# Polysketch attention followed by an ELU feed-forward layer: the order of the first loads, sketch products and features

## The chip, the cores and the metric

The kernel runs on one core of a Trainium2 chip. The metric is device time in microseconds of one execution. Below, "the profile" and "the trace" are of one execution, recorded by the hardware profiler; times in it count from the start of its span. PE is TensorE's matmuls, DVE is VectorE, ACT ScalarE, POOL GpSimd, SP SyncE (which issues most DMAs). All arithmetic is in float32.

## The reference, cut to what matters

q, k and v have the shape (4, 4, 1088, 32): 4 batches, 4 heads, 1088 positions, head dimension 32. S1 and S2 are (8, 32), w_in is (128, 2048), w_out (2048, 128). The sketches and the weights come in as 64-bit floats, q, k and v as float32.

```python
def phi(x):
    a = np.einsum('rd,bhsd->bhsr', S1, x)
    b = np.einsum('rd,bhsd->bhsr', S2, x)
    return np.einsum('bhsi,bhsj->bhsij', a, b).reshape(*x.shape[:-1], r * r)
q_p, k_p = (phi(q), phi(k))
kv = np.einsum('bhsf,bhsd->bhfd', k_p, v)
z = np.sum(k_p, axis=2)
num = np.einsum('bhsf,bhfd->bhsd', q_p, kv)
den = np.einsum('bhsf,bhf->bhs', q_p, z)[..., None] + 1e-06
x = num / den                      # then to (4352, 128)
h = x @ w_in
g = np.where(h > 0.0, h, 1.0 * (np.exp(np.minimum(h, 0.0)) - 1.0))
return g @ w_out
```

## The kernel before, in words

The order of the work on each engine is written out by hand: the program is in manual schedule, and each engine carries out its instructions in the order in which the code emits them. Waits between engines follow from the tiles that are written and read. A tile of a pool with n buffers waits until the n-th tile before it under the same tag has been read.

**Tokens and groups.** The 4352 tokens are cut into half tiles of 64 (17 per batch), and eight of these make a group: groups 0 to 8, the last one smaller. The FFN runs over groups, and in each over 8 pairs cp of 128-column chunks of the hidden layer. One step (g, cp) has two matmuls h = w_in x (`mm1`, L606), two activations per half on ScalarE (`elu_a`, L622 and L624), one VectorE operation per half (`elu_d`, L630, writes gg) and two matmuls with w_out that add into o (`mm2`, L643), two steps behind. The loop at L801 does this for all steps and hangs the attention of batches 1 to 3 and of later groups between them. Everything ahead of it, L680 to L727, is the head: it works out batch 0's keys and the first two groups, and starts the FFN.

**Loads.** SP issues nearly all. The order is S1, k and q of batch 0 in parts (the ScalarE queue issues S2 and the second half of k and q), then v of batch 0 (`load_v(0)`, L141, two DMAs of 288 and 256 KB), then raw w_in of pair 0 (`load_w(0, 0)`, L182, 256 KB), the tail of q of batch 0 (L183), and further weights. Each DMA signals on one of eight semaphores in turn, and one on the same semaphore waits for the one before.

**Rounding of the weights.** w_in and w_out come as 64-bit words; each float64 is turned into a float32 by five steps, `round_a` to `round_e` (L97 to L124): round_a on VectorE (L98), round_b on ScalarE (L103), round_c (two VectorE operations, L111 and L112), round_d (L116), round_e (L124, on VectorE or GpSimd). `RA(i)` and `RB(i)` are the first two for entry i of the list `order` (L163), `RC(i)` the other three. Entry 0 is w_in of pair 0, entry 1 w_in of pair 1, entries 2 and 3 their w_out.

**Sketches.** S16 holds S1 and S2 rounded, Sx their copies per head. `sps` (L250) gives Sab, the sketch matrices of all heads on the diagonal, masked on VectorE (L252). SXps (L237, in `make_SXh`) gives SXh through a copy on ScalarE (L238) and a mask on GpSimd (L239); it turns batch 0's sums into the weights of the denominators.

**The head, in its order.** `transp` (L230) turns keys and queries on VectorE. `KF(0)` (L280) multiplies 18 half tiles of keys with Sab into abp; in it, after five matmuls, stands `make_SXh`. Two ScalarE copies bring abp to abk (L297). `q1_first` (L440) is the same for the queries of group 0 (abqp, copied to abq at L449). `KO_first` (L336, VectorE) and `KO_pool` (L271, GpSimd) form the outer products kp. `Z_first` (L397): products for the sums z (zps, L349), their copy zl on ScalarE (L372), the product with SXh (Z, L377), the masked result in SW (`Z_out`, L381). `q1z_first` (L452) multiplies the queries with it (zqp), `q2_den` (L506) forms the denominators on VectorE (pw L513, den L516, L517, an L519), `q2_out` (L522) the outer products qp in two halves (L530) and takes a function `then` that is called behind the first half. `KA(0)` (L359) multiplies kp with v into kv, `KS_first` (L407) copies it (kd, L409), transposes it (L410) and copies again (kvS, L411). `q4_early` (L535) transposes qp on TensorE (qtp, L544), four at a time, and copies each four on ScalarE (qpT, L545). `q5_early` (L547) multiplies with kvS (xps, L551) and copies to xg, the FFN's x (L557): for group 0 both copies on ScalarE, for group 1 the second on VectorE. `mm1_first` (L608) is mm1 for (0, 0) in two blocks, one per half w of xg (L613). `q1_second` (L461) multiplies group 1's queries with SW (abwp, L466) and copies them to abw (ScalarE, L470); `q2(1)`, `q4_early(1)` and `q5_early(1)` follow for group 1 as for group 0.

**Fillers.** `keep_warm(n, cols)` (L214) is n matmuls of a constant tile whose result nobody reads (tile idle, L216). PSUM tiles of tag aux have two buffers: qtp, xps and abwp among them.

Of the kernel before, what the change touches and what calls it, by code (L numbers as in the profile page):

```python
# [12 lines left out]
F32 = mybir.dt.float32  # L13
# [14 lines left out]
def kernel(  # L28
# [20 lines left out]
    nc = tc.nc  # L49
    B, H, S, D = q.shape  # L50
    R = S1.shape[0]
    P = 128
# [4 lines left out]
    NT = S // 64  # L57
# [16 lines left out]
    def load_hd(eng, x, src, b, t0, t1, c=slice(0, 2)):  # L74
        if (x, b) not in hd:
            hd[x, b] = work.tile([P, 2, NT, D], F32, name="hd_" + x, tag="hd_" + x)
        eng.dma_start(hd[x, b][:, c, t0:t1, :],
                      src[b].rearrange("h (a c t) d -> (h a) c t d", a=32, c=2)[:, c, t0:t1, :])

    def load_v(b, engs=(nc.sync, nc.sync)):  # L80
        for u, eng in enumerate(engs):
            t0, t1 = u * KT, min(NT, u * KT + KT)
            r = slice(64 * u, 64 * u + 64)
            src = v[b].rearrange("h (y t) d -> y h t d", t=NT)[:, :, t0:t1, :]
            eng.dma_start(vt[b][r, :VN].rearrange("p (h t d) -> p h t d", h=H, t=KT)[:, :, :t1 - t0, :], src)
# [52 lines left out]
    load_hd(nc.scalar, "k", k, 0, KT, NT)  # L138
    load_hd(nc.sync, "q", q, 0, 0, 8, slice(0, 1))
    load_hd(nc.scalar, "q", q, 0, 0, 8, slice(1, 2))  # L140
    load_v(0)  # L141
    warm = const.tile([R, 1], F32, name="warm")
    nc.vector.memset(warm[:], 0.0)  # L143
    nc.scalar.activation(warm[:], warm[:], EXP)
# [4 lines left out]
    def load_w(cp, i):  # L149

        f = slice(2 * cp * P, (2 * cp + 2) * P)
        src = moe_w_out[f, :].rearrange("(c p) d -> p c d", p=P) if i else moe_w_in[:, f]
        if wide:
            if cp not in raw_w:
                raw_w[cp] = work.tile([P, 4 * P, 2], U32, name="raw", tag="raw", bufs=6)
            src = src.bitcast(U32)
            to = raw_w[cp][:, 2 * P * i:2 * P * i + 2 * P, :].rearrange("p c w -> p (c w)")
        else:
            to = W[:, cp, 2 * P * i:2 * P * i + 2 * P]
        nc.sync.dma_start(to.rearrange("p (c f) -> p c f", f=src.shape[-1]) if i else to, src)  # L160
# [10 lines left out]
    def RA(i):  # L171
        round_w(round_a, i)

    def RB(i):
        round_w(round_b, i)
# [4 lines left out]
        round_w(round_e, i, pool)  # L180

    load_w(0, 0)  # L182
    load_hd(nc.sync, "q", q, 0, 8, NT)  # L183
    load_w(1, 0)
    load_w(1, 1)
# [28 lines left out]
    def keep_warm(n, cols=256):  # L214
        for i in range(n):
            nc.tensor.matmul(idle[:, :cols], some[:, :P], some[:, :cols], skip_group_check=True)  # L216
# [18 lines left out]
    def make_SXh():  # L235
        xps = psum.tile([P, 512], F32, name="SXps", tag="aux")
        nc.tensor.matmul(xps[:, :FD], idr[:].rearrange("p x j -> p (x j)"), Sx[:R].rearrange("p h d -> p (h d)"))  # L237
        nc.scalar.copy(SXh[:], xps[:, :FD])  # L238
        nc.gpsimd.tensor_mul(SXh[:].rearrange("p (h d) -> p h d", h=H), SXh[:].rearrange("p (h d) -> p h d", h=H),  # L239
                             _ap(hmask[:], [[1, H], [0, D]]))  # L240
# [7 lines left out]
    keep_warm(1, 96)  # L248
    sps = psum.tile([P, 512], F32, name="sps", tag="aux")
    nc.tensor.matmul(sps[:, :2 * R], Sx[:].rearrange("p h d -> p (h d)"), ident[:2 * R, :2 * R])  # L250
    keep_warm(1)
    nc.vector.tensor_mul(Sab[:], _ap(sps[:, :2 * R], [[0, H], [1, 2 * R]]), _ap(bmask[:], [[1, H], [0, 2 * R]]))  # L252
    nc.gpsimd.tensor_copy(SW[:, :, :2, :].rearrange("p h x r -> p h (x r)"), Sab[:])
# [26 lines left out]
    def KF(b):  # L280
        ps = [psum.tile([P, 512], F32, name="abp", tag="h", bufs=4) for _ in range(2)]

        part = [(range(5), 0), (range(3), 1)]
        todo = [(i, u) for r, u in part for i in r] + [x for i in range(5, KT) for x in ((i - 2, 1), (i, 0))]
        todo += [(i, 1) for i in range(KT - 2, KT)]
        for n, (i, u) in enumerate(todo):
            if n == 5:
                make_SXh()
            nc.tensor.matmul(ps[i // 5][64 * u:64 * u + 64, 64 * (i % 5):64 * (i % 5) + 64],  # L289
                             kT[b][:, u * KT + i, :], Sab[:].rearrange("p h y -> p (h y)"),  # L290
                             skip_group_check=True, tile_position=(0, 64 * u))
        kf_ps.extend(ps)
        ab = feats[b] = work.tile([P, 2, KT, H, R], F32, name="abk", tag="abk", bufs=2)
        for j in range(2):
            t = slice(0, 5) if j == 0 else slice(5, KT)
            n = t.stop - t.start
            nc.scalar.copy(ab[:, :, t].rearrange("p x t h r -> p x (t h) r"),  # L297
                           ps[j][:, :64 * n].rearrange("p (m x r) -> p x m r", x=2, r=R))
# [98 lines left out]
    def Z_first():  # L397
        ps = psum.tile([P, 512], F32, name="zps", tag="h", bufs=4)
        for i in range(KT):
            z_tile(0, ps, i)  # L400
        zl = ZC(0, ps)
        keep_warm(1, 160)
        Z(0, ps, zl)
        Z_out(0, ps)
        keep_warm(1, 160)
# [46 lines left out]
    def q1z_first():  # L452
        p = psum.tile([P, 512], F32, name="zqp", tag="h", bufs=4)
        for i in range(4):
            for u in range(2):
                b, t = half_tile(0, 2 * i + u)
                nc.tensor.matmul(p[64 * u:64 * u + 64, i * 32:i * 32 + 32].rearrange("p (h r) -> p h r", h=H),
                                 qT[b][:, t, :], SW[:, :, 2, :], skip_group_check=True, tile_position=(0, 64 * u))
        return p[:, :128].rearrange("p (t h r) -> p h t r", t=4, h=H)
# [46 lines left out]
    def q2_den(g, zq=None):  # L506
        m = H * qn[g]
        x = abw[g][:, :m, :]
        pw = pws[g % 2]
        if zq is None:  # L510
            nc.vector.tensor_mul(pw[:, :m, :R], x[:, :, R:2 * R], x[:, :, 2 * R:3 * R])
        else:
            nc.vector.tensor_mul(pw[:, :m, :R].rearrange("p (h t) r -> p h t r", h=H),  # L513
                                 x[:, :, R:2 * R].rearrange("p (h t) r -> p h t r", h=H), zq)
        den = work.tile([P, 4 * H], F32, name="den", tag="den")
        nc.vector.tensor_reduce(den[:, :m], pw[:, :m], axis=AX, op=ADD)  # L516
        nc.vector.reciprocal(den[:, :m], den[:, :m])  # L517
        an = work.tile([P, 4 * H, R], F32, name="an", tag="an")
        nc.vector.tensor_mul(an[:, :m], x[:, :, R:2 * R], _ap(den[:, :m], [[1, m], [0, R]]))  # L519
        ans[g] = an  # L520

    def q2_out(g, parts=1, then=None):  # L522
        m = H * qn[g]
        x, an = abw.pop(g), ans.pop(g)
        qp[g] = work.tile([P, 4 * H, R, R], F32, name="qp", tag="qp", bufs=2)
        for i in range(parts):
            h = slice(i * m // parts, (i + 1) * m // parts)
            a_ = an[:, h]
            b_ = x[:, h, :R]
            nc.vector.tensor_mul(qp[g][:, h], _ap(a_, list(a_.ap[1:]) + [[0, R]]),  # L530
                                 _ap(b_, [b_.ap[1], [0, R], b_.ap[2]]))
            if then and i == 0:
                then()

    def q4_early(g):  # L535

        qpT[g] = work.tile([P, H, 2, P], F32, name="qpT", tag="qpT", bufs=2)
        for hh in range(2):
            p = psum.tile([P, 512], F32, name="qtp", tag="aux")
            for h2 in range(2):  # L540
                for m in range(2):
                    o = (h2 * 2 + m) * P
                    r = (2 * hh + h2) * 4 + 2 * m
                    nc.tensor.transpose(p[:, o:o + P], qp[g][:, r:r + 2].rearrange("p t i j -> p (t i j)"), ident[:])  # L544
            nc.scalar.copy(qpT[g][:, 2 * hh:2 * hh + 2], p[:].rearrange("p (h m s) -> p h m s", h=2, m=2))  # L545
# [59 lines left out]
        for c in cs:  # L605
            nc.tensor.matmul(hs[g, cp][c][:, :n], W[:, cp, c * P:c * P + P], xg[g][:, :n])  # L606

    def mm1_first(w):  # L608
        if w == 0:
            hs[0, 0] = [psum.tile([P, 512], F32, name="h", tag="h", bufs=4) for c in range(2)]  # L610
        for c in range(2):
            cols = [x[:].rearrange("p (m w s) -> p w m s", w=2, s=P)[:, w] for x in (hs[0, 0][c], xg[0])]
            nc.tensor.matmul(cols[0], W[:, 0, c * P:c * P + P], cols[1], skip_group_check=True)  # L613

    def elu_a(g, cp, c, parts=(0, 1)):

# [69 lines left out]
    KO_pool()  # L686
    Z_first()
    zq = q1z_first()
    q2_den(0, zq)
    q2_out(0, 2, lambda: RA(0))  # L690
    KA(0)
    KS_first()
    RB(0)
    keep_warm(1, 256)
    keep_warm(1, 128)
    q4_early(0)
    RA(1)
    RB(1)
    RC(0)
    q5_early(0)  # L700
    transp(qT, "q", 0, 8, NT)
    mm1_first(0)
    RA(2)
    RB(2)
    q1_second()
    mm1_first(1)
    RC(1)
    round_w(round_c, 2)
    elu_a(0, 0, 0)
    elu_a(0, 0, 1)  # L710
    mm1(0, 1)
# [1 line left out]
    q4_early(1)  # L713
    for c in range(2):
        elu_d(0, 0, c)
    RA(3)
    RB(3)
    round_w(round_d, 2)
# [70 lines left out]
    for g in range(2, NQ):  # L789
        n = NP * (g - 1)  # L790
# [60 lines left out]
```

## Time and profile before

| what | value |
|---|---|
| five executions, us | 282.84, 280.65, 280.34, 283.43, 283.45 |
| median, us | 282.84 |
| the profiled execution: its time | 282.84 |
| its span | 280.9 |
| instructions | 4933 |
| PE busy | 275.0 us, 98% of the span |
| PE weight loads | 139.0 us, 49% |
| DVE busy | 179.2 us, 64% |
| ACT busy | 181.6 us, 65% |
| POOL busy | 14.5 us, 5% |
| HBM read, written | 10.88 MB, 2.23 MB |
| DMA | 13.42 MB, mean 48 GB/s |

The busy time of matmuls is no measure of how well they are used: they are pipelined, and fillers count. A float32 matmul shows as two records. The chain of work that ended last is found by going back from the last instruction: at each step to what released it, or to the instruction before it on its engine. Time that an engine is on this chain is time that the span is made of. In the timelines each row has start, duration, engine, line, operation and out<-in with the shapes; rows of one kind that follow each other are merged (xN).

### The profile page before, as it was taken

How to read it: one execution, taken by the hardware profiler on the slowest of the kernel's cores; microseconds unless marked ns; L12 is line 12 of the kernel's file. 1: busy time of each engine (PE TensorE's matmuls, PEld its weight loads, DVE VectorE, ACT ScalarE, POOL GpSimd, SP SyncE). 2: the span in 40 equal slices, each digit the busy share in tenths (PEclk: the TensorE clock that was granted, in tenths of full speed). 3: DMA queues.
4: the chain of work that ended last, by engine and by line, in shares of the span. 5: the costliest groups of instructions: out<-in, count | busy, mean ns of one | idle time of the engine just before them, and what ended most of it. 6: DMA issues, size and time to landing. Idle time of an engine off the chain costs nothing.

```text
span 280.9 us, 4933 instructions
## 1 busy us (share of the span) xinstructions
PE 275.0 (98%) x1913; PEld 139.0 (49%) x1913; DVE 179.2 (64%) x336; ACT 181.6 (65%) x352; POOL 14.5 (5%) x39
## 2 busy tenths in 40 slices
PE   8989999999999999999999999999999999999995
PEld 6854444454444444444544454445444454444694
DVE  6498899996959784668545653566445744562442
ACT  2268968686566467666566666665666666667682
POOL 3500006300000000000000000000000000000000
PEclk9999999999999999999999999999999999999999
DMA  6993772200002200001000100020002000100020
GB/s 179 341 330 97 254 217 62 82 0 2 0 2 43 36 0 2 0 13 27 3 0 15 23 2 2 2 37 0 2 0 37 1 2 0 25 12 2 4 36 19
DMA packets 25638, 13.42 MB, mean 48 GB/s; under 512 B 18448, under 2 KB 23824, under 8 KB 25616
## 3 DMA queue, kind: packets, MB, share of 16 engines
q1 hardware_dynamic: 25024, 12.66, 17.8%
q10 hardware_dynamic: 592, 0.46, 0.5%
q8 instruction: 15, 0.25, 0.4%
q14 instruction: 7, 0.06, 0.1%
HBM read 10.88 MB, written 2.23 MB: 47 GB/s over the span
## 4 chain that ended last, share of the span: by engine, by line
PE 98%; ACT 1%; DVE 0%; issue 0%
PE h L606 41%; PE o L643 40%; PE ol L666 3%; PE idle L216 2%; PE kv L359 2%; PE h L572 1%; PE abp L289 1%; PE qps L572 1%; PE h L490 1%; PE h L613 1%; PE xps L551 1%; PE kfps L308 1%; PE qtp L544 1%; PE qps L490 1%; ACT qpT L545 0%; PE abwp L466 0%
## 5 line engine op out<-in xcount | busy, mean ns | idle before, releaser
L630 DVE SCALAR_TENSOR_TENSOR gg<-e,h 128x512 f32<-128x512 f32 (+1 forms) x144 | 93.0, 654 | 83.0 <-ACT e L624 82.8
L606 PE MATMUL h<-xg,W 128*128 128x512 f32 (+1 forms) x284 | 126.8, 569 | 0.1
L622 ACT ACTIVATE e<-h 128x512 f32<-128x512 f32 (+1 forms) x144 | 81.6, 567 | 64.8 <-PE h L606 64.6
L643 PE MATMUL o<-gg,W 128*128 128x512 f32 x256 | 121.5, 597 | 0.0
L624 ACT ACTIVATE e<-e 128x512 f32<-128x512 f32 (+1 forms) x144 | 87.3, 606 | 4.6
L606 PEld LDWEIGHTS h<-xg,W 128*128 128x128 f32 x284 | 53.4, 190 | 61.9 <-issue 49.7
L643 PEld LDWEIGHTS o<-gg,W 128*128 128x128 f32 x256 | 47.3, 190 | 55.6 <-issue 54.3
L530 DVE TENSOR_TENSOR qp<-an,abw 128x1024 f32<-128x1024 f32 (+1 forms) x9 | 9.3, 1047 | 0.3
L103 ACT ACTIVATE W<-W,ebias 128x256 uint32<-128x256 uint32 (+1 forms) x11 | 6.6, 603 | 3.4 <-DVE W L98 3.4
L572 PE MATMUL h<-qpT,kvq 32*32 32x128 f32 (+1 forms) x256 | 8.7, 257 | 0.0
L572 PE MATMUL qps<-qpT,kvq 32*32 32x128 f32 (+1 forms) x224 | 8.7, 271 | 0.0
L216 PE MATMUL idle<-some 128*128 128x256 f32 (+3 forms) x20 | 7.1, 487 | 1.2 <-DVE warm L143 1.2
L666 PEld LDWEIGHTS ol<-W,gg 128*128 128x128 f32 x64 | 8.1, 192 | 0.3
L563 DVE STREAM_TRANSPOSE qpT<-qp 128x1024 f32<-128x1024 f32 (+1 forms) x7 | 8.1, 1161 | 0.0
L666 PE MATMUL ol<-W,gg 128*128 128x128 f32 x64 | 8.1, 275 | 0.0
L584 ACT COPY xg<-h 128x128 f32<-128x128 f32 (+1 forms) x14 | 2.9, 261 | 7.8 <-PE qps L572 5.5
L572 PEld LDWEIGHTS h<-qpT,kvq 32*32 32x32 f32 x256 | 5.4, 103 | 4.7 <-issue 3.8
L111 DVE SCALAR_TENSOR_TENSOR W<-raw,W 128x256 uint32<-128x256 uint32 (+1 forms) x11 | 7.6, 693 | 0.0
L500 DVE STREAM_TRANSPOSE abw<-h 128x128 f32<-128x128 f32 (+1 forms) x14 | 3.5, 288 | 4.8 <-ACT xg L584 4.8
L271 POOL TENSOR_TENSOR kp<-abk 128x1024 f32<-128x1024 f32 (+1 forms) x3 | 6.5, 2165 | 1.8 <-ACT abk L297 1.8
L116 DVE SCALAR_TENSOR_TENSOR raw<-raw 128x256 f32<-128x256 uint32 (+1 forms) x11 | 6.0, 549 | 0.3
L359 PEld LDWEIGHTS kv<-kp,v 128*32 128x32 f32 x288 | 4.8, 110 | 2.3 <-issue 1.5
(115 smaller groups left out, 153.6 us busy)
## 6 DMA issues: line engine op xcount, KB each, us to landing
raw<-in_moe_w_in_dram SPq DMA_DIRECT2D x8, 256.0 KB, 5.9
raw<-in_moe_w_out_dram SPq DMA_DIRECT2D x8, 256.0 KB, 6.1
hd_k<-in_k_dram SPq DMA_DIRECT2D x3, 544.0 KB, 8.2
hd_q<-in_q_dram SPq DMA_DIRECT2D x3, 544.0 KB, 3.4
out_dram<-ob SPq DMA_DIRECT2D x40, 32.0 KB, 1.7
v<-in_v_dram SPq DMA_DIRECT2D x4, 288.0 KB, 6.5
v<-in_v_dram SPq DMA_DIRECT2D x4, 256.0 KB, 6.6
hd_k<-in_k_dram SPq DMA_DIRECT2D x1, 288.0 KB, 3.5
```

Source lines behind the costliest of these rows:

```text
L111: nc.vector.scalar_tensor_tensor(d, hi, 0x80000000, d, op0=AND, op1=OR)
L216: nc.tensor.matmul(idle[:, :cols], some[:, :P], some[:, :cols], skip_group_check=True)
L359: nc.tensor.matmul(kv[32 * h:32 * h + 32, :R * R], vt[b][:, (h * KT + i) * D:(h * KT + i + 1) * D], kp[i // 5][:, i % 5, h].rearrange("p i ...
L530: nc.vector.tensor_mul(qp[g][:, h], _ap(a_, list(a_.ap[1:]) + [[0, R]]), _ap(b_, [b_.ap[1], [0, R], b_.ap[2]]))
L563: nc.vector.transpose(qpT[g][:, :m].rearrange("p m f s -> p (m f s)"), qp[g][:, :m].rearrange("p m i j -> p (m i j)"))
L572: nc.tensor.matmul(ps[c][D * h:D * h + D, 64 * k:64 * (k + m)], kvq[r, b, f, h, :], qpT[g][r, n * h + 2 * k:n * h + 2 * (k + m), f, :], st ...
L606: nc.tensor.matmul(hs[g, cp][c][:, :n], W[:, cp, c * P:c * P + P], xg[g][:, :n])
L622: nc.scalar.activation(e, hs[g, cp][c][:, :n], RELU, scale=-1.0)
L624: nc.scalar.activation(e, e, EXP, scale=-1.0)
L630: nc.vector.scalar_tensor_tensor(gs[g, cp][:, c, :n], es[g, cp][:, c, :n], -1.0, hs[g, cp][c][:, :n], op0=ADD, op1=MAX)
L643: nc.tensor.matmul(ops[g][:, :n], W[:, cp, (2 + c) * P:(3 + c) * P], gg[:, c, :n], start=(first and c == 0), stop=(last and c == 1))
L666: nc.tensor.matmul(ops[g][i][:], gg[:, c, i * P:i * P + P], W[:, cp, (2 + c) * P:(3 + c) * P], start=(first and c == 0), stop=(last and c ...
```

## The change

Seven edits, all in the head:

- `load_v(0)` is issued behind `load_w(0, 0)` instead of ahead of it.
- `make_SXh()` is called directly behind the product sps, ahead of a filler, instead of inside `KF` after five matmuls.
- In `Z_first` the filler of 160 columns between the copy zl and the product Z is left out; the one behind Z stays.
- `RA(0)` goes from between the halves of `q2_out(0)` to ahead of `q2_den(0)`; `RB(0)` from behind `KS_first` to behind `q2_den(0)`. `q2_out` loses its argument `then`.
- Behind `RB(0)`'s old place the filler of 128 columns is left out; the one of 256 stays.
- The transposition of the rest of batch 0's queries goes ahead of `RA(1)`; `q1_second()` goes ahead of `mm1_first`, whose two blocks become one call.
- `round_c` of entry 2 goes from ahead of `elu_a(0, 0, 0)` to behind `elu_d(0, 0, c)`.

```diff
     load_hd(nc.scalar, "q", q, 0, 0, 8, slice(1, 2))
-    load_v(0)
     warm = const.tile([R, 1], F32, name="warm")
...
     load_w(0, 0)
+    load_v(0)
     load_hd(nc.sync, "q", q, 0, 8, NT)
...
     nc.tensor.matmul(sps[:, :2 * R], Sx[:].rearrange("p h d -> p (h d)"), ident[:2 * R, :2 * R])
+    make_SXh()
     keep_warm(1)
...
-        for n, (i, u) in enumerate(todo):
-            if n == 5:
-                make_SXh()
+        for i, u in todo:
             nc.tensor.matmul(ps[i // 5][64 * u:64 * u + 64, 64 * (i % 5):64 * (i % 5) + 64],
...
         zl = ZC(0, ps)
-        keep_warm(1, 160)
         Z(0, ps, zl)
         Z_out(0, ps)
         keep_warm(1, 160)
...
-    def q2_out(g, parts=1, then=None):
+    def q2_out(g, parts=1):
...
-            if then and i == 0:
-                then()
...
-    def mm1_first(w):
-        if w == 0:
-            hs[0, 0] = [psum.tile([P, 512], F32, name="h", tag="h", bufs=4) for c in range(2)]
-        for c in range(2):
-            cols = [x[:].rearrange("p (m w s) -> p w m s", w=2, s=P)[:, w] for x in (hs[0, 0][c], xg[0])]
-            nc.tensor.matmul(cols[0], W[:, 0, c * P:c * P + P], cols[1], skip_group_check=True)
+    def mm1_first():
+        hs[0, 0] = [psum.tile([P, 512], F32, name="h", tag="h", bufs=4) for c in range(2)]
+        for w in range(2):
+            for c in range(2):
+                cols = [x[:].rearrange("p (m w s) -> p w m s", w=2, s=P)[:, w] for x in (hs[0, 0][c], xg[0])]
+                nc.tensor.matmul(cols[0], W[:, 0, c * P:c * P + P], cols[1], skip_group_check=True)
...
     zq = q1z_first()
+    RA(0)
     q2_den(0, zq)
-    q2_out(0, 2, lambda: RA(0))
+    RB(0)
+    q2_out(0, 2)
     KA(0)
     KS_first()
-    RB(0)
-    keep_warm(1, 256)
-    keep_warm(1, 128)
+    keep_warm(1)
     q4_early(0)
+    transp(qT, "q", 0, 8, NT)
     RA(1)
     RB(1)
     RC(0)
     q5_early(0)
-    transp(qT, "q", 0, 8, NT)
-    mm1_first(0)
+    q1_second()
+    mm1_first()
     RA(2)
     RB(2)
-    q1_second()
-    mm1_first(1)
     RC(1)
-    round_w(round_c, 2)
     elu_a(0, 0, 0)
     elu_a(0, 0, 1)
     mm1(0, 1)
...
     for c in range(2):
         elu_d(0, 0, c)
+    round_w(round_c, 2)
     RA(3)
```

## The prediction

> **What bounds the kernel now.** I read the page's chain of work first, then that chain in order of time for the first 33 us, then the timelines of VectorE, TensorE and ScalarE over the same stretch. The page's fourth part:
>
> ```profile
> PE 98%; ACT 1%; DVE 0%; issue 0%
> PE h L606 41%; PE o L643 40%; PE ol L666 3%; PE idle L216 2%; PE kv L359 2%; PE h L572 1%; PE abp L289 1%; PE qps L572 1%; PE h L490 1%; PE h L613 1%; PE xps L551 1%; PE kfps L308 1%; PE qtp L544 1%; PE qps L490 1%; ACT qpT L545 0%; PE abwp L466 0%
> ```
>
> TensorE carries the end: behind about 26 us its matmuls (L606, L643) run back to back. So a microsecond won in the head, before the FFN runs steadily, moves all that follows and is worth one microsecond; an idle VectorE or ScalarE later is worth nothing. The change touches only the head. The chain there, in order of time (start, us, what):
>
> ```profile
> 4.49 0.54 PE sps L250 x2
> 5.02 1.15 PE idle L216 x2
> 6.17 1.26 PE abp L289 x10
> 7.43 0.72 PE SXps L237 x2
> 8.16 1.79 PE abp L289 x23
> ...
> 15.27 0.45 PE qtp L544 x4
> 15.72 0.07 issue
> 15.80 0.64 PE qtp L544 x4
> 16.44 0.02 issue
> 16.46 0.59 ACT qpT L545
> 17.06 0.04 issue
> 17.10 0.76 PE xps L551 x14
> 17.86 0.36 ACT xg L557
> 18.22 0.04 issue
> 18.26 1.13 PE h L613 x4
> 19.39 0.81 PE abwp L466 x16
> 20.20 1.06 PE h L613 x4
> 21.26 1.72 PE h L606 x4
> ```
>
> Up to 13.9 us TensorE is occupied without a gap, fillers (idle) included; from 14 to 18.3 us the chain hops between TensorE, VectorE (qp) and ScalarE. VectorE around the second product qp (start, us, line, operation):
>
> ```profile
> 14.15 0.69 DVE L530 TENSOR_TENSOR qp<-an,abq 128x512 f32<-128x512 f32 x1
> 14.76 0.29 DVE L98 TENSOR_SCALAR W<-raw 128x256 uint32<-128x256 uint32 x1
> 14.96 0.68 DVE L530 TENSOR_TENSOR qp<-an,abq 128x512 f32<-128x512 f32 x1
> ```
>
> The reader should see that RA(0) (L98) stands between the halves of qp: the second starts 0.81 us after the first, where back to back it would be 0.61 (14.76 - 14.15). Its end, 14.96 + 0.68 = 15.64, releases the second four transposes at 15.80.
>
> **The change, part by part.**
>
> *Load order.* w_in of pair 0 (256 KB) is issued ahead of v (544 KB) on SP; bytes and number of DMAs stay. DMA is at 1.0 share from 4 us on, so v lands later by about what 256 KB cost: the loads that follow land some 0.7 us apart (10.85, 11.68, 12.41, 13.15), so v's halves go from 7.67 and 8.67 to about 8.4 and 9.4. KA reads v at 12.7: over 3 us of cover. Raw w_in landed by about 9.4 before (SP's issue waiting for a semaphore came free then), and RA(0) wants it at 11.7. Both orders suffice: 0 us. If the cover were gone, KA would start later by the overshoot. The two q and w transfers behind keep their places, and nobody else on SP waits.
>
> *SXps directly behind sps.* It leaves the abp block, where it costs 0.72 on the chain, and stands ahead of the one filler, so the first abp moves from 6.17 to about 6.9. Its inputs are ready: idr at 3.42, Sx at 4.14. What abp waits for is no later: Sab ends at 5.28, the first kT piece at 5.70. Moved work alone gains 0; but abp is no longer broken up. The break spans 7.12 (last pass started) plus 0.11 (pitch) to 8.09, 0.86 us against 0.72. I take 0.14, between 0 and 0.3 (one more such changeover). POOL does SXh before SW's copy; SW is first read 12 us later.
>
> *Filler of 160 columns before Z removed.* zl ends at 11.30, Z starts at 11.44 behind the filler. Without it 0.05 remains (kd 14.24 to its transpose 14.29): 0.09, of which ScalarE's abq copy, which waits for the later end of abqp, gives up some 0.03. Bounds 0 and 0.14. SW, zqp and pw are then 0.2 earlier (pw 12.81 to 12.6).
>
> *RA(0) ahead of q2_den, RB(0) ahead of kd.* RA(0) (0.29) goes into the 0.76 us for which VectorE waits for zqp; RB(0) (0.51) into ScalarE's wait of 2.68 us ahead of kd. The halves of qp close up: 0.20. With the 0.2 above, qp ends at 15.24, and the second transposes start at 15.40. The first must go early too, or ScalarE takes the place of VectorE: the filler of 128 columns that held them until 15.11 is gone (two passes, 0.22), so they start near 14.7, behind qp's first half (14.62). qpT's second copy goes from 16.46 to 16.06, xg's first from 17.84 to 17.44. Bounds 0.1 and 0.5 at this point; I take 0.4.
>
> *q1_second (abwp) ahead of mm1_first.* abwp now waits for its PSUM slot, which xg's first copy frees: nearly the same event that released L613 before, so TensorE restarts at 17.86 instead of 18.26 and only the order changes. The q transposition (0.77) moves ahead of RA(1) and RC(0) on VectorE: qT is ready near 15.9, W of pair 0 near 17.7 (17.44 before; wanted at 18.65, cover 0.9). The two L613 blocks become one. Four passes of 256 columns at the pace of L606 (1.72 for four of 512) are 0.86; the chain gives 1.13 and 1.06, so a block pays 0.2 to 0.27 for its start, now once. I take 0.2 (0 to 0.27). L606 goes from 21.26 to about 20.65: 0.6 in all.
>
> *Group 1.* abw is copied at 18.8 instead of 20.25, so VectorE's q2 starts at about 19.4 instead of 20.76 and ends near 22.0 instead of 23.40. TensorE reaches the second qtp block at 22.35; its second half no longer waits for qp (23.40, then 23.55 before). ScalarE is then the next in the row: two qpT copies at 0.51 pitch instead of the 0.60 between 23.61 and 24.21: 0.09 more. What is late next: round_c(2) (0.75) is moved behind gg, so VectorE has gg until 23.4, round_c to 24.05, RA(3), round_d to 24.65, and its xg copy is wanted at 24.9; on ScalarE, RB(3) runs 24.3 to 24.8 and xg follows at 24.9. Both just fit; if not, up to 0.3 is given back.
>
> **Sum:** 0.14 + 0.06 + 0.20 + 0.20 + 0.09 = 0.69, about 0.7 us by 26 us, bounds 0 and 1.1. The profiled execution has a span of 280.9 and a time of 282.84, which is also the median of the five; so span 280.2 and 282.1 us.
>
> **A rate that changes in the head.** Two rows of the TensorE timeline:
>
> ```profile
> 4.95 1.22 PE L216 MATMUL idle<-some 128*128 128x256 f32 x2
> 25.44 0.70 PE L216 MATMUL idle<-some 128*128 128x256 f32 x2
> ```
>
> The same two passes take 1.22 and 0.70, and small matmuls change pace near 10.2 us (abp 0.107 apart before, abqp 0.058 after), though the granted-clock column reads 1.00. The five times lie in two groups, 280.34 and 280.65, and 282.84, 283.43 and 283.45: means 2.7 apart. If the rate rose at 5 us instead of 10.2, half of 5.2 us of path would go, 2.6 us; I infer, and do not know, that this is the difference.
>
> The Trainium skill ("TensorE: Matmul & The Clock Gate", Part 1: The HAM clock gate) says that the clock doubles after about 3.4 us of sustained activity, judged over a free-running window, so that the moment differs from run to run; this trace shows the rise only after 9 us of work. An estimate by the page would have the rise at latest two windows after 1.19, at 8.0, and abp's and SXps' saving at half, so 0.6 instead of 0.7.
>
> **The rivals.**
>
> *Nothing is won* (282.8, from 282.5 to 283.4). RB(3) and xg on ScalarE, or the packed VectorE between gg and xg, give back what the head gained, or abwp's wait costs more than its order saves. For it: the cover of 0.1 to 0.25 us there. Against: the gain ahead of it is already 0.6, and an overshoot of that size needs each of five VectorE operations to be 0.1 longer than in its row.
>
> *The median falls into the lower group* (280.50 - 0.7 = 279.8). For it: two of five were there, and nothing in the change touches the first 4.9 us. Against: three of five were not, and SXps's half-filled 0.72 us moves to an earlier point, which can count against an early rise as well as help a later one.
>
> *Slower: the rate falls back.* Two fillers, 0.27 and 0.22 us, leave TensorE idle around 11 and 14.5 us. Price: the slow stretch at the start lasted 9 us; as long a one from 11.3 on, with TensorE busy 0.66 to 1.00, costs 3 to 4.5 us less what was won, 285 to 286.6; one of a third that length, 283.5. It decides where a microsecond is less busy than 0.66: at 17 to 18 us TensorE was that idle (0.66, then 0.74) and 256 columns stayed at the quick pace. So little speaks for it.
>
> **How the numbers follow.** The forecast, a shift of 0.4 to 1.0 with the median in the upper group, 0.55; nothing won, 0.18; lower group, 0.21; rate falls back, 0.06. Predicted 282.1, its own range 281.7 to 282.5. The range over the cases: 279.6 to 283.2 holds the forecast, the lower group nearly whole and most of "nothing won". One per cent is 2.83 us, about what a measurement of this kernel can tell from no change. Below 280.0 lies three quarters of the lower group, 0.16; above 285.7 half of the last rival, 0.03; within, 0.81.
>
> **What would show it.** Right: RA(0) ahead of pw and the qp halves 0.61 apart; transposes' second half near 15.4; abwp at 17.9 directly behind xps and one block of eight L613-type passes behind it; q2 of group 1 near 19.4; the L606-type block 0.5 to 0.8 earlier near 25.5, and as much off the span. Wrong: a wait for xg or RB(3) near 25 us; v waited for at KA; fillers of 256 columns at 0.43 a pass behind 11 us; or a rise of the rate at another time than 10.2, which would hide the 0.7 altogether.

## The result and the profile after

The changed kernel takes 281.54 us (median of 43 runs, 279.42 to 284.54), the kernel before 282.91 (median of 80). The ratio is 0.9958 with a 95% interval of 0.9939 to 0.9977: 0.42% less time, about 1.2 us. The forecast was 282.1, in a range of 279.6 to 283.2, with 0.74 us or 0.26% off. So the sign and that range hold, and the gain is larger than forecast: 1.2 us by the ratio and 1.37 by the medians. The narrower range of the forecast by itself, 281.7 to 282.5, is missed by 0.16 us. The profiled execution has a span of 279.4 and a time of 281.33. One of the 43 runs, 284.54, and three single runs below (290.25, 360.01, 407.68) show a mean clock of 0.988, 0.948, 0.761 and 0.662 where the others have 0.994 or more, and no group below counts them.

The chain is still TensorE's; line numbers are shifted by up to five. First the first line of the page's fourth part, then the chain in the head in order of time, of the kernel after:

```profile
PE 97%; ACT 1%; issue 0%; DVE 0%
```

```profile
5.02 0.61 PE SXps L237 x2
5.64 1.15 PE idle L216 x2
6.79 2.49 PE abp L288 x33
...
14.21 0.56 PE qtp L540 x4
14.77 0.02 issue
14.79 0.64 PE qtp L540 x4
15.43 0.02 issue
15.45 0.59 ACT qpT L541
...
16.85 0.36 ACT xg L553
17.21 0.04 issue
17.25 0.88 PE abwp L464 x16
18.13 1.92 PE h L609 x8
20.06 1.72 PE h L602 x4
```

Set beside the chain of before: abp, which was 10 records in 1.26 us, SXps, then 23 in 1.79, is now 33 in 2.49. xg's first copy is on the chain at 16.85 instead of 17.86 (1.01 earlier), the first L606-type block (L602 now) at 20.06 instead of 21.26 (1.20 earlier), and the one that follows group 1's features at 24.73 instead of 26.20 (1.47 earlier). The span is 1.5 us shorter: all that was won in the head arrives at the end.

VectorE of the kernel after, around RA(0) (L98) and the halves of qp, in one row now:

```profile
11.01 0.19 DVE L380 TENSOR_TENSOR SW<-zps,bmask 128x32 f32<-128x32 f32 x1 [0.28 <-PE zps L376]
11.12 0.93 DVE L98 TENSOR_SCALAR W<-raw 128x256 uint32<-128x256 uint32 x1
11.96 0.28 DVE L511 TENSOR_TENSOR pw<-abq,zqp 128x128 f32<-128x128 f32 x1
...
13.35 1.29 DVE L528 TENSOR_TENSOR qp<-an,abq 128x512 f32<-128x512 f32 x2
```

The halves take 1.29 together, against 14.96 + 0.68 - 14.15 = 1.49 before: the 0.20 is there. But RA(0) took 0.93 us instead of 0.29, and that was not foreseen.

### The profile page after: what moved, and what is told of

The parts are those of the page before. It is cut to its first block, busy times and chain, and to the rows that moved or that the text cites. A ratio compares the mean times of both kernels' runs of the same rounds, so it can differ in the third digit from the quotient of the medians.

```text
span 279.4 us, 4925 instructions
## 1 busy us (share of the span) xinstructions
PE 273.1 (98%) x1909; PEld 137.9 (49%) x1909; DVE 180.0 (64%) x336; ACT 181.4 (65%) x352; POOL 14.5 (5%) x39
## 4 chain that ended last, share of the span: by engine, by line
PE 97%; ACT 1%; issue 0%; DVE 0%
PE h L602 41%; PE o L639 40%; PE ol L662 3%; PE idle L216 2%; PE kv L358 2%; PE h L568 1%; PE qps L568 1%; PE abp L288 1%; PE h L488 1%; PE kfps L307 1%; PE h L609 1%; PE xps L547 1%; PE qtp L540 1%; PE qps L488 1%; ACT qpT L541 0%; PE abwp L464 0%
## 5 line engine op out<-in xcount | busy, mean ns | idle before, releaser
L602 PE MATMUL h<-xg,W 128*128 128x512 f32 (+1 forms) x284 | 126.8, 569 | 0.1
L602 PEld LDWEIGHTS h<-xg,W 128*128 128x128 f32 x284 | 53.4, 190 | 61.9 <-issue 49.7
L216 PE MATMUL idle<-some 128*128 128x256 f32 (+2 forms) x16 | 6.3, 531 | 1.2 <-DVE warm L142 1.2
```

## The experiments

**The times of one kernel lie in groups.** Before: 280.3 to 280.9 (31 of 80 runs), 282.7 to 283.1 (17), 283.4 to 284.1 (32). After: 279.4 to 280.4 (10 of 43) and 281.1 to 282.0 (32). A median hangs on how many runs fall in which group, so below, groups are compared with groups. Each trace records when the clock of TensorE goes to its full rate (a table follows).

**SXps alone, behind sps, in the kernel before.**

```diff
-            if n == 5:
-                make_SXh()
...
     nc.tensor.matmul(sps[:, :2 * R], Sx[:].rearrange("p h d -> p (h d)"), ident[:2 * R, :2 * R])
+    make_SXh()
     keep_warm(1)
```

> The kernel before with SXps alone moved directly behind sps. Theory A (the recorded step's mechanism with another size): the product in the middle of abp kept its two 64-row streams from running beside each other, so KF's last product starts 0.6 to 0.75 us earlier than in the kernel before (9.95 there), and KA starts 0.6 to 0.8 earlier (12.69 there); time 0.6 to 0.8 below the kernel before within the same group of times. Rival B (the size on record, 0.14): 0.1 to 0.2 earlier at both places, 0.1 to 0.2 off the time; the rest of what the changed kernel won by KA came from the matmul rate that rose at 9.1 instead of 10.2 us.

Measured: 280.62 us (median of 12; ratio 0.9947, 0.9910 to 0.9983), in groups 280.1 to 280.7 and 281.9 to 282.0. The last abp starts at 9.06 (9.95 before) and KA at 11.68 (12.69 before). In the lower group 0.3 is won (medians 280.33 against 280.64 of the kernel before beside it), and the upper group is 0.8 to 2 us below the two upper groups of before. In the trace theory A holds at both places (0.89 and 1.01 earlier, of which the rise, at 8.79 instead of 10.21, has a part), and 0.14 was too small by far. In time the lower group's 0.3 lies between the two theories; in such runs, by the rises of the table below, the clock is at its full rate before abp begins, and the break costs less. The price is plain in the chain of this kernel:

```profile
5.02 0.61 PE SXps L237 x2
5.63 1.15 PE idle L216 x2
6.79 2.33 PE abp L288 x33
```

33 records of abp in 2.33 us are 0.07 each; the ten ahead of SXps in the kernel before took 0.126 each, the 23 behind it 0.078. The ten belong to the five products that the code emits first, and all five write the same half of abp's partitions; the first products for the other half come behind SXps. Single records of the two traces show what the break does. In the kernel before, the ten start 0.107 apart (the first two 0.16), then the break takes 0.97 from start to start, and the five records behind it are again 0.107 apart or more; only from there on do two start in every 0.107 for most of the way. Without the break two start in 0.107 from the eighth record on. So the slow beginning comes twice, and the two halves run beside each other for less of the way. I read it so: SXps takes the whole width of the array, and the two 64-column streams cannot run beside each other across it. The paces are measured, this reading of them is not.

**RA(0) and RB(0) alone, with the filler of 128 columns dropped, in the kernel before.**

```diff
+    RA(0)
     q2_den(0, zq)
-    q2_out(0, 2, lambda: RA(0))
+    RB(0)
+    q2_out(0, 2)
...
-    RB(0)
-    keep_warm(1, 256)
-    keep_warm(1, 128)
+    keep_warm(1)
```

> The kernel before with RA(0) ahead of q2_den, RB(0) behind it and the filler of 128 columns dropped, nothing else. Theory A: the two halves of qp start 0.61 apart instead of 0.81, RA(0) costs VectorE nothing ahead of pw, and xg's first copy comes 0.15 to 0.25 earlier counted from pw; time 0.2 lower. Rival B: RA(0), which took 0.93 instead of 0.29 us in the changed kernel, holds pw back and takes 0.2 or more of it away again; time unchanged.

Measured: 283.17 us (median of 12; ratio 1.0024, 0.9986 to 1.0062), nothing that the time can tell: only one of 12 runs was in the lower group. The trace tells it: qp's halves start 0.61 apart, and from the first half to xg's first copy it is 3.48 us (3.68 before), the 0.20 of theory A. Its groups, 282.65 to 283.0 and 283.4 to 283.8, lie about 0.2 and 0.4 below those of before by their medians, and its one run in the lower group 0.1. RA(0) took 0.30 here, since it began after GpSimd's product kp was done.

**The order of group 1 alone, in the kernel before.**

```diff
     q4_early(0)
+    transp(qT, "q", 0, 8, NT)
     RA(1)
...
-    transp(qT, "q", 0, 8, NT)
+    q1_second()
     mm1_first(0)
+    mm1_first(1)
     RA(2)
     RB(2)
-    q1_second()
-    mm1_first(1)
     RC(1)
-    round_w(round_c, 2)
...
         elu_d(0, 0, c)
+    round_w(round_c, 2)
```

> The kernel before with only the order of group 1 changed: the transposition of the queries ahead of RA(1), abwp ahead of both mm1_first blocks, round_c of entry 2 behind gg. Theory A (step 5 and 6 on record): 0.2 for the one block of L613 and 0.1 to 0.3 for the second qtp block that no longer waits for qp; 0.3 to 0.5 counted from xg's first copy to the first L606 of (1, 0), and as much off the time. Rival B: abwp waits for the slot that xg's copy frees and VectorE is packed behind gg, so under 0.1 is left.

Measured: 282.95 us (median of 12; ratio 0.9999, 0.9952 to 1.0046); lower group 280.04 to 280.25 against 280.42 to 280.75 of the kernel before beside it, about 0.45 less by the means. In its trace it is 9.69 us from xg's first copy to the first product with w_out (L643), against 10.16 before and 9.69 in the changed kernel: 0.47. Theory A. The median alone would have called this step worthless. In the lower group the three single edits, 0.3, 0.1 (one run) and 0.45, add up to about what the whole change wins there, 0.9.

**v first again, in the changed kernel.**

```diff
+    load_v(0)
     warm = const.tile([R, 1], F32, name="warm")
...
     load_w(0, 0)
-    load_v(0)
```

> The changed kernel with v loaded ahead of raw w_in as before. Theory A: w_in lands near 9.4, RA(0) wants it near 11.1, v is wanted near 11.9, so the time is that of the changed kernel within 0.1 in the same group of times. Rival B: the load order is what feeds RA(0) in time and lets the head run; without it RA(0) or pw comes later by 0.2 or more and the time rises by as much.

Measured: 279.72 us (median of 12; ratio 0.9916, 0.9878 to 0.9954), with 8 of 12 runs in the lower group. Group by group (279.48 to 279.79 and 281.70 to 281.94) it is the changed kernel. In its trace, where the rate rose at 5.08, RA(0) does wait for the load:

```profile
9.65 0.60 DVE L98 TENSOR_SCALAR W<-raw 128x256 uint32<-128x256 uint32 x1 [0.24 <-DMA raw<-in_moe_w_in_dram]
10.17 0.29 DVE L511 TENSOR_TENSOR pw<-abq,zqp 128x128 f32<-128x128 f32 x1
```

The load order takes this wait of 0.24 away, and it is worth nothing: RA(0) ends at 10.25 here, when GpSimd's kp lets it, early or late begun.

**The changed kernel itself, on the chip of the next three.**

> The changed kernel itself, beside the next three on one chip. Theory A (the groups of times are set by the moment at which the matmul rate rises, which lies on a grid of 3.41 us that does not start with the kernel): the same two groups, about 279.4 to 280.4 with a rise at 4 to 5 us and 281.1 to 282.0 with a rise near 7.5 to 9.2 us, in shares that no edit of loads changes; so the version with v first is the same kernel in time, group by group, within 0.1. Rival B: v first has a larger share of early rises (8 of 12 there), because the load order moves the start against that grid; then this one shows 3 or fewer of 12 in the lower group.

Measured: 281.58 us (median of 12; ratio 0.9935, 0.9898 to 0.9971): four runs at 279.4 to 280.5, seven at 281.3 to 282.0. By the bound that was set, 3 or fewer of 12, rival B is not met. Over all its chips the changed kernel had 14 of 53 in the lower group, against 8 of 12 with v first on one chip; chance alone gives such a difference about once in 65. Without the filler ahead of abp the shares are 4 of 11 with v first and 3 of 12 with w_in first, on different chips. So whether the load order shifts the shares stays open.

**Without the leading fillers, in the changed kernel.**

```diff
-    keep_warm(3)
-    keep_warm(1, 96)
```

> The changed kernel without the four leading fillers (three of 256 columns and one of 96), which fill 1.19 to 4.42 us ahead of sps; sps waits for Sx at 4.14 in any case. Theory A: without them no stretch ahead of sps is busy, the rate cannot rise at 4 to 5 us, and the group at 279.4 to 280.4 disappears: all runs at 281.1 or above, some near 283 to 284.5. Rival B: the groups come from elsewhere (loads, memory), and the lower group stays.

Measured: 281.57 us (median of 12; ratio 0.9960, 0.9927 to 0.9993), all 12 runs at 281.0 to 282.1. The lower group is gone, the upper one is where it was. Theory A: the lower group needs the busy stretch from 1.19 to 4.42 us, and the upper one does not. At the changed kernel's share of 14 in 53, twelve runs without one in the lower group would come by chance about once in 40.

**Without the filler between SXps and abp, in the changed kernel.**

```diff
     make_SXh()
-    keep_warm(1)
     nc.vector.tensor_mul(Sab[:], ...
```

> The changed kernel without the filler of 256 columns between SXps and abp. Theory A: the filler holds abp back: Sab ends at 5.3 and the first kT piece at 5.7, so abp starts near 5.75 instead of 6.72 and, where the rate has not risen, everything behind is 0.5 to 0.9 earlier, 0.1 to 0.3 where it rose at 4 to 5 us. Rival B: the filler is needed to let the rate rise at 7.5 to 9.2; without it the rise slips by one step of 3.41 us, and the late group lands 0.5 to 1.5 higher.

Measured: 280.62 us (median of 12; ratio 0.9937, 0.9902 to 0.9972): 279.5 to 280.05 (3 runs) and 280.56 to 281.15 (9). The changed kernel's upper group on the same chip was 281.26 to 281.96: 0.7 to 0.9 less, and the two do not overlap. Theory A for the late rises; in the lower group, where it expected 0.1 to 0.3, nothing is shown (279.44 to 280.51 beside it). TensorE in this kernel (here the rate rose at 4.93):

```profile
4.87 0.49 PE L237 MATMUL SXps<-Sx,idr 8*128 8x128 f32 x2
5.76 1.73 PE L287 MATMUL abp<-Sab,kT 128*64 128x64 f32 x36 [0.40 <-DVE kT L230]
```

abp now waits 0.40 for the first kT piece and starts at 5.76 instead of 6.72. Group by group no version that keeps this filler has an upper group as low by its median. By median it beats both kernels, but the version with v first has the lowest of all, 279.72, by its share of early rises, and the interval of the ratio here overlaps that of the changed kernel.

**SXps back in abp, in the changed kernel.**

```diff
-    make_SXh()
     keep_warm(1)
...
+        for n, (i, u) in enumerate(todo):
+            if n == 5:
+                make_SXh()
```

> The changed kernel with SXps back in the middle of abp, all else changed. Theory A: abp's streams are broken again (last abp about 0.7 later when the rate is low, 0.3 when it is high), and some runs rise only at 13 us: the lower group 0.3 above that of the changed kernel, the upper one at 282 and above and with a third group near 283. Rival B (0.14 on record): 0.1 to 0.2 above in every group and no third group.

Measured: 282.35 us (median of 12; ratio 0.9991, 0.9949 to 1.0034): 280.2 to 280.3 (3), 282.1 to 282.8 (6), 284.3 (3). The last abp is back at 10.00. Three groups return: the lower two lie 0.4 and 0.7 below those of the kernel before by their medians, near what the other edits won alone, and the third lies 0.5 above, later than theory A had it and not explained. Theory A in the main: without this step the rest cannot be told from no change by the ratio, and the step carries some 0.7 us where the rate rises late and 0.3 to 0.6 where it rises early.

**The filler of 160 columns put back ahead of Z, in the changed kernel** (one execution):

```diff
         zl = ZC(0, ps)
+        keep_warm(1, 160)
         Z(0, ps, zl)
```

> The changed kernel with the filler of 160 columns put back between zl and Z. Theory A (step on record): Z starts 0.09 later behind zl's end than without the filler. Rival B: in the traces so far Z starts 0.145 behind zl's end with the filler (before) and without it (after), so the filler lies wholly in a wait that is there anyway: 0.145 again, nothing won by leaving it out.

Measured: zl ends at 10.41, Z starts at 10.55: 0.144 with the filler; 0.145 in the kernels before and after. Time 281.29, in the middle of the changed kernel's upper group. Rival B, at this rate: the filler lay in a wait that is there anyway. TensorE's rows, with the filler at 10.11:

```profile
10.11 0.54 PE L216 MATMUL idle<-some 128*128 128x160 f32 x2
10.55 0.38 PE L376 MATMUL zps<-zl,SXh 128*128 128x32 f32 x2
```

At the low rate it is otherwise. In the kernel before with RA and RB moved, whose rate rose at 13.35, the same filler takes 0.90 and zl ends at 11.80, but Z starts at 12.21:

```profile
11.51 0.90 PE L216 MATMUL idle<-some 128*128 128x160 f32 x2
12.21 0.47 PE L377 MATMUL zps<-zl,SXh 128*128 128x32 f32 x2
```

There the filler held Z back by 0.26 (0.403 behind zl instead of 0.145). So leaving it out is worth nothing where the rate has risen by about 10 us, and something in the runs in which it has not.

**Both: no filler ahead of abp, v first.** The diffs of the two versions above together.

> The changed kernel without the filler between SXps and abp, and with v loaded ahead of raw w_in as before. Theory A: load order is worth nothing, so the times are those of the version without that filler: a lower group at 279.4 to 280.1 and an upper one at 280.5 to 281.2, 0.6 to 0.9 below the upper group of the changed kernel. Rival B: v first moves the early rises to about two thirds of the runs, median below 280.

Measured: 280.61 us (median of 11; ratio 0.9927, 0.9887 to 0.9966): four runs at 279.35 to 279.49, six at 280.53 to 281.09, one at 282.51. Theory A: the same kernel in time as with w_in first.

**No filler ahead of abp, and no leading filler of 96 columns.**

```diff
     keep_warm(3)
-    keep_warm(1, 96)
```

> The changed kernel without the filler between SXps and abp and without the leading filler of 96 columns. Theory A: sps starts 0.14 earlier (Sx is ready at 4.14, the fillers held TensorE until 4.42), Sab and abp with it, so the upper group is 0.1 to 0.2 below that of the version that keeps the 96 columns (280.56 to 281.15). Rival B: abp then waits for the first kT piece, whose load lands at 4.9 to 5.0, so nothing is won; or less busy time ahead of sps takes early rises away, and the lower group is gone.

Measured: 280.87 us (median of 8; ratio 0.9914, 0.9876 to 0.9953), one run at 279.45 and seven at 280.55 to 281.42. sps did start 0.12 earlier (4.30), abp at 5.61, but nothing is won. In the profiled execution (281.42) the chain goes through a load, not through sps:

```profile
2.06 6.14 DMA hd_q<-in_q_dram
8.20 0.02 issue
8.22 0.72 DVE qT L230
```

The queries' load, 6.14 us from its issue, was late here. That is rival B in another place (q, not kT), but for this execution only: q landed at 8.20, in the other twelve traces at 6.17 to 7.58, and without the filler ahead of abp (abp at 5.76) qT began at 6.67 and nothing waited. What held the other seven runs is not known.

**When the rate rises, and what the time is then.** From the traces, the record at which TensorE's clock goes to full, and the time of the same execution:

| kernel | rise, us | time, us |
|---|---|---|
| before | 10.21 | 282.84 |
| before + RA and RB | 13.35 | 283.80 |
| before + group 1 | 4.17 | 280.04 |
| before + SXps | 8.79 | 281.90 |
| after, SXps back | 10.48 | 282.28 |
| after | 9.14 | 281.33 |
| after, again | 4.70 | 279.44 |
| after, v first | 5.08 | 279.65 |
| after, 160 columns back | 9.06 | 281.29 |
| after, no leading fillers | 8.62 | 281.00 |
| after, no filler ahead of abp | 4.93 | 279.54 |
| after, no filler ahead of abp, v first | 4.08 | 279.37 |
| after, neither filler ahead of abp nor 96 columns | 9.73 | 281.42 |

Every execution of a lower group has its rise at 4 to 5.1 us, every other at 8.6 or later. From the rise to the fall at the end it is 269.65 us before and after and in six more, 273.07 in the other five: 79 and 80 times 3.413. So rise and fall lie on one grid of that step, whose place differs from run to run.

## Why the prediction was right or wrong

The sign and the path were right, and the sum was too small by more than half: it gave 0.69 where the head won 1.47. The result lies below the forecast's own range; it lies within the whole range because that was made wide enough to hold the lower group. The terms of its sum, and what the two profiled executions show, counted by how much earlier things happen after each step:

| step | on record | in the traces |
|---|---|---|
| SXps behind sps | 0.14 | 0.73 at the last abp |
| filler ahead of Z | 0.06 | 0; another 0.12 by KA from the rise |
| RA(0), RB(0) | 0.20 | 0.16 (1.01 in all at xg) |
| one L613-type block | 0.20 | 0.19 (1.20 in all) |
| group 1 | 0.09 | 0.27 (1.47 in all) |
| sum | 0.69 | 1.47 |

*What bounds the kernel* was right: the chain behind 26 us did not change, and the 1.47 us of the head are the 1.5 by which the span is shorter.

*SXps directly behind sps* is the term that was mis-sized. Its mechanism was named ("abp is no longer broken up"), but its cost was read as one changeover of the row, 0.14, with 0.3 for a bound. The chain of before already showed more: ten records in 1.26 us ahead of the break, 23 in 1.79 behind it. Had the ten run at the pace of the 23, 0.48 would have been saved. 0.14 + 0.48 = 0.62, near the 0.73 of the trace. Of the rest the earlier rise (9.14 against 10.21) can have only a small part at this place, where two records of abp start behind 9.14; it accounts for the 0.12 of the next row, where the 13 abqp records take 0.62 instead of 0.74. How much of the rise is the edit's doing and how much the place on the grid, two executions cannot tell.

*The second half of that step was not foreseen at all*: the record saw two groups in five runs, and there are three. In the kernel before 32 of 80 runs lie at 283.4 to 284.1; the one trace of such a time, of the version with RA and RB moved (283.80), has its rise at 13.35. In the changed kernel the latest group ends at 282.0, and with SXps alone moved none of 12 runs is above 282.02; with SXps back, three of 12 are at 284.3. So this step takes the latest group away. That it does so because a denser abp lets the rate rise one grid step sooner is an inference; it was not measured by itself. The groups' cause, on record as an inference, is borne out by the table of rises, in which early rises and low times go together without exception, and by the kernel without leading fillers.

*The filler ahead of Z*: 0.05 was taken from the wait of another transposition (kd to its transpose, 0.054). Here the wait is 0.145 with the filler and without it; only at the low rate, at 13.35, did the filler cost 0.26.

*RA(0)*: "goes into the 0.76 us for which VectorE waits" held by luck. GpSimd's kp ran until 11.89 and held RA(0) until 12.05; pw, which overlaps its end, still started at 11.96, 0.05 behind zqp's end (11.92), as it did before (12.76 and 12.81). With a kp that is a little later, pw would have waited. The qp halves won their 0.20; 0.04 was lost again ahead of them, where `an` took 0.34 instead of 0.29.

*Load order*: 0 was right, the cover was not: "wants it at 11.7" is true where the rate rises late; at a rise of 5 us RA(0) wants it at 9.41 and w_in in the old place lands at 9.6. The queries' second half, which no step counted, landed at 6.25 to 6.99 in the six traces with v first and at 6.17 to 8.20 in the seven with w_in first; whether the order does this is not shown.

*Group 1*: the size was off since one of two gains was left out. The second qtp block's wait for qp (0.16) and the closer qpT copies (0.48 apart instead of 0.60) add up; the record counted the second alone, at 0.09. xg and RB(3) were as tight as it said: RB(3) began at 23.70, a 0.37 us wait, and xg's copies at 24.11 and 24.15 still met the L602 block at 24.73.

*The rivals.* "Nothing is won" did not come. Of "the median falls into the lower group", the size was near (medians of the lower groups 280.56 before and 279.6 after, 0.9 apart) and its share not: 10 of 43. "The rate falls back" did not come: fillers could go, and the version with one filler less has a lower upper group still.

**The rule about the clock.** The record weighed the Trainium skill's page "TensorE: Matmul & The Clock Gate" (Part 1: The HAM clock gate): a doubling after about 3.4 us of sustained work, on a free-running window. The runs agree with the grid (3.413) and with a moment that differs from run to run; they do not agree with the record's estimate from it, a rise at the latest two windows after the first work, at 8.0: in seven traces with TensorE in work from 1.19 the rise came at 8.79 to 13.35. How much work in a window counts as sustained, no run here shows.

## What to carry to other kernels

A small product over the whole array in the middle of products that use half of it each can cost more than its own time, here about 0.6 us more: compare the time per product ahead of the break and behind it before costing the move. Where executions of one kernel lie in groups, look for the record at which TensorE's clock rises, and compare group with group and step with step in the trace; here a step of 0.45 us had a ratio of 0.9999 over all runs. Fillers are worth a trial each: none of the 12 runs without the leading ones was among the fastest, while one of 256 columns only held the keys' products back, by about 0.7 us where the rate rises late.

## What the hardware showed that was not expected

RA(0), a VectorE operation on a 128x256 tile in SBUF, takes 0.29 us alone and up to 0.93 beside GpSimd's product kp. VectorE's row is shown above; GpSimd's in the kernel after is this:

```profile
9.94 1.96 POOL L272 TENSOR_TENSOR kp<-abk 128x1024 f32<-128x1024 f32 x1 [3.23 <-ACT abk L296]
```

kp ends at 11.89, RA(0) at 12.05; with v first at 10.10 and 10.25; without leading fillers at 11.57 and 11.72. In each of the eight traces where the two overlap RA(0) takes 0.55 to 0.93 and ends 0.15 behind kp, whenever it began. The Trainium skill's page "SBUF — State Buffer" (SBUF: two separate sides) says that VectorE, in a two-port mode or with two inputs in SBUF, and GpSimd share a pair of ports under an exclusive lock, held for a whole instruction, and that the other one fully blocks. These ends agree with it; in which mode RA(0) runs, no trace shows. The SW product of 0.19 just ahead of RA(0), which reads PSUM, was not held up.
